# Prologue filler matmuls split into eight tiles of 64 rows by 32 columns, in a fused attention and MLP block

## The chip, the cores and the metric

The kernel runs on one core of one Trainium2 chip. The metric is the device time of one execution in microseconds, the median of three runs. A core has five engines that run their own instruction lists side by side and meet through semaphores: TensorE (PE in the profile; its weight loads are listed as PEld), VectorE (DVE), ScalarE (ACT), GpSimd (POOL) and SyncE (SP), which issues most DMAs. PE writes its results to PSUM, which has eight banks of 512 fp32 columns on 128 partitions; DVE and ACT read them from there. A matmul on PE is a pair of instructions: a weight load (LDWEIGHTS, the stationary operand) and the matmul itself, which streams the other operand through the array column by column.

## The reference

One layer norm feeds an attention with 32 query heads on one shared key and value head, and an MLP; both are added to the input.

```python
xn = _layernorm(x)                              # (1, 2048, 512), bf16
q = (xn @ wq).reshape(B, S, 32, 16)             # 32 heads of 16
k, v = xn @ wk, xn @ wv                         # one head of 16
p = softmax(q @ k.T * 16 ** -0.5)
a = (p @ v).reshape(B, S, 512) @ wo
h = gelu(xn @ w1 + b1)                          # 512 -> 1792
return x + a + h @ w2 + b2
```

## The kernel before

The kernel is straight-line code. Its functions do not issue instructions; they record operations with the tiles they read and write, a rough length and a due time (`Prog.add`). `Prog.schedule` then runs a planner: it simulates the engines, picks for each one the operation to put next, and so fixes the order of every engine's list; `Prog.emit` works out the semaphore waits and writes the lists. On the chip each engine works through its list in that order.

There are two parts in time.

The prologue (some 24 us) loads x in eight DMAs on SP's queue (line 770, two row tiles of 128 each), and behind them the weights wq, w1, w2. DVE and ACT take the statistics of the 16 row tiles (lines 851 to 877), DVE, ACT and POOL normalise them into `xn` (lines 887 and 891), PE transposes them (line 910, four transposes of 128x128 a tile), and ACT and DVE move the transposes from PSUM banks 0 to 2 to `xnT` (lines 915 and 917). From `xnT` PE projects K (line 741, 128x512, into bank 4), V and K in rows (line 741, 128x32, the kind "v") and the first query group (into bank 7). DVE's statistics are in a fixed list; a tile waits there for the DMA that brings it.

The body (all the rest) works through units of three score tiles: PE makes scores (line 1080, three row tiles of 32 rows), ACT takes their exponential (line 1104) or DVE makes an integer approximation of it (line 1135), and PE multiplies with V (line 1148, column tiles of 128 rows by 32 columns). The MLP and the projections are put into PE's gaps.

The fillers. While not all "v" matmuls of the prologue are placed, the planner puts a filler on PE where it has nothing else to place, from planner time 2.0 us on (`PRO_FROM`), as long as its count of PE activity in the last 3.413 us (`WIN`) is below 0.8 of that (`FILL_U`). It counts a filler as 0.107 us of activity, and as long as 0.107 us, or twice that while its model has PE slow. A filler multiplies a tile of zeros with itself and writes to PSUM bank 3, which nothing reads before line 1003. It waits for the zeros and for nothing else. The planner places 29 of them, in rows of 16, 9, 1, 1 and 2. In a later place of the body there are other fillers (line 1515 before), which the change does not touch.

Which instructions stand between the rows of fillers on PE: 4 transposes after the row of 16, 4 after the row of 9, 8 after the next one, 8 "v" matmuls after the next one, and after the last two the rest of the prologue, beginning with 8 transposes whose first waits for POOL.

Of the kernel before, what the change touches and what calls it, by code (L numbers as in the profile page):

```python
# [612 lines left out]
def bass_parallel_sum__grouped_kv_mqa__dense_activation_gelu__prompt_kernel(  # L613
# [33 lines left out]
    with ExitStack() as es:  # L647
        def sb(shape, dtype, name):
            return es.enter_context(nc.sbuf_tensor(name, shape, dtype))
# [20 lines left out]
        zeros = sb([P, P], bf, "zeros")  # L670
# [45 lines left out]
        def bank(b, n=1):  # L716
            return pAll[:, b * 512:(b + n) * 512]

        pO, pM = bank(6), bank(7)
        pr = Prog(nc)  # L720
# [53 lines left out]
        for i in range(8):  # L774
            e = X_Q[i]
# [734 lines left out]
        pr.in_chain = False  # L1510
        if PRO_FROM:
            zr = bass.AP(zeros[:].tensor, zeros[:].offset, [list(zeros[:].ap[0]), [0, 2], [1, P]])
            pr.pro_filler = lambda e: e.matmul(bank(3)[:, 0:256], zeros[:], zr, start=True, stop=True, skip_group_check=True)
        if FILL_GAP:
            pr.filler = lambda e, j, o: e.matmul((pO if o else pM)[32 * j:32 * j + 32, :], zeros[:, 0:32], xnT[:, 0, 0:TBW],
                                                 start=not o, stop=not o, skip_group_check=True,
                                                 tile_position=(0, 32 * j))
# [37 lines left out]
```

## Time and profile before

| | us |
|---|---|
| median of 3 runs | 730.26 (730.18 to 730.27) |
| the profiled execution | 730.02 |
| its span, first to last instruction | 728.2 |
| PE matmuls busy | 713.9 (98%) |
| PE weight loads busy | 223.5 (31%) |
| DVE busy | 691.4 (95%) |
| ACT busy | 712.8 (98%) |
| POOL busy | 418.2 (57%) |
| mean granted clock of PE | 0.997 |

A matmul's time in the profile runs from its start until its result is through, and matmuls overlap in the array, so a PE that is 98% busy is not full; start-to-start distances tell more. In the chain of waits each line is a start, a length and the work that the end of the kernel stood on at that time. In a timeline the bracket at a line's end is the idle time of that engine before it and what ended it. "PEclk", or the column before the DMA share in the table of windows, is the clock that PE was granted as a share of full speed. DMA queue q1 carries the transfers of SP, q8 and q14 instructions.

### The profile page before, as it was taken

To read this page: it belongs to the slowest core of one execution; us is meant where nothing else is said; L and a number is where in the kernel's file an instruction comes from. 1 tells how busy PE (TensorE), PEld (TensorE's weight loads), DVE (VectorE), ACT (ScalarE), POOL (GpSimd) and SP (SyncE) were. 2 spreads that over 40 slices of the span, in tenths; PEclk is the share of its full clock that TensorE was granted. 3 is DMA by queue.
4 is the path that set the end of the run, shared out by engine and by line. 5 is a ranking of instruction groups with operands and counts; after the bars stand their busy time and mean duration, and the time that the engine had idled before them with its cause. 6 is when DMAs were issued, how large, how long until landed. Compare 5 with 4: busy or idle time off the path is not lost.

```text
span 728.2 us, 22534 instructions
## 1 busy us (share of the span) xinstructions
PE 713.9 (98%) x9301; PEld 223.5 (31%) x9301; DVE 691.4 (95%) x1243; ACT 712.8 (98%) x757; POOL 418.2 (57%) x669
## 2 busy tenths in 40 slices
PE   7999999999999999999999999999999999999998
PEld 5333332232242323222222233222333222232332
DVE  8799999999999889999999999999999999999685
ACT  7899999999999999999999999999999999999997
POOL 8445567667665243667777754445663767755131
PEclk9999999999999999999999999999999999999999
DMA  9200101001010110110101021100101101011111
GB/s 312 72 13 18 29 9 25 17 13 29 9 40 9 28 44 18 23 34 10 30 14 32 14 48 30 28 20 9 29 7 25 27 22 25 16 40 32 26 29 39
DMA packets 36253, 23.59 MB, mean 32 GB/s; under 512 B 17768, under 2 KB 32568, under 8 KB 36152
## 3 DMA queue, kind: packets, MB, share of 16 engines
q1 hardware_dynamic: 35096, 22.12, 11.6%
q8 instruction: 74, 1.21, 0.7%
q14 instruction: 27, 0.22, 0.1%
q10 hardware_dynamic: 1056, 0.03, 0.1%
HBM read 13.28 MB, written 2.35 MB: 21 GB/s over the span
## 4 chain that ended last, share of the span: by engine, by line
ACT 55%; PE 37%; DVE 7%; DMA 1%; issue 0%; POOL 0%; SPq 0%
ACT E L1104 55%; PE pAll L1148 18%; PE pAll L1080 11%; PE pAll L765 4%; DVE Dt L1135 3%; PE pAll L747 2%; DVE Dt L1188 2%; PE pAll L741 1%; DVE stats L854 1%; DMA x_sb<-in_A_x_dram 1%; PE pAll L910 0%; PE pAll L761 0%; DVE x_sb L1314 0%; DVE qp L1280 0%; DVE Dt L1156 0%
## 5 line engine op out<-in xcount | busy, mean ns | idle before, releaser
L1104 ACT ACTIVATE E<-pAll 128x1024 bf16<-128x1024 f32 (+2 forms) x675 | 662.4, 1154 | 2.1 <-PE pAll L1080 0.6
L1155 POOL INT64_ADD Dt<-Dt x603 | 396.2, 666 | 289.9 <-DVE Dt L1135 116.2
L1135 DVE TENSOR_SCALAR Dt<-pAll 128x512 int16<-128x512 f32 (+2 forms) x570 | 394.1, 711 | 21.5 <-PE pAll L761 16.1
L1148 PE MATMUL pAll<-Dt,V 128*32 128x512 bf16 x3010 | 413.2, 383 | 0.7 <-DVE Dt L1188 0.2
L1148 PE MATMUL pAll<-E,V 128*32 128x512 bf16 x1446 | 280.1, 385 | 0.0
L1080 PE MATMUL pAll<-QT,KT 32*128 32x512 bf16 x2048 | 267.0, 384 | 5.3 <-ACT E L1104 3.6
L1188 DVE TENSOR_SCALAR Dt<-Dt 128x1024 int16<-128x1024 int16 (+4 forms) x302 | 202.4, 680 | 1.4 <-PE pAll L1148 0.7
L1080 PEld LDWEIGHTS pAll<-QT,KT 32*128 32x128 bf16 x2048 | 66.6, 90 | 273.9 <-ACT E L1104 246.7
L1148 PEld LDWEIGHTS pAll<-Dt,V 128*32 128x32 bf16 x3010 | 106.0, 94 | 114.0 <-issue 77.3
L1148 PEld LDWEIGHTS pAll<-E,V 128*32 128x32 bf16 x1446 | 65.5, 94 | 51.4 <-issue 39.7
L765 PE MATMUL pAll<-xnT,w_sb 128*32 128x512 bf16 x520 | 80.7, 383 | 0.3 <-DVE ub L1314 0.3
L1156 DVE TENSOR_SCALAR Dt<-Dt 128x1024 int16<-128x1024 int16 (+1 forms) x147 | 46.9, 341 | 0.1
L765 PE MATMUL pAll<-w_sb,x_sb 128*32 128x512 bf16 x304 | 46.5, 382 | 0.0
L765 PE MATMUL pAll<-w_sb,ub 128*32 128x512 bf16 x352 | 45.4, 382 | 0.0
L761 PE MATMUL pAll<-w_sb,ub 32*128 32x512 bf16 x96 | 36.9, 385 | 0.0
L765 PE MATMUL pAll<-wop,oTp 128*32 128x512 bf16 x192 | 34.9, 383 | 0.0
L761 PE MATMUL pAll<-w_sb,x_sb 32*128 32x512 bf16 x88 | 33.8, 384 | 0.1
L761 PE MATMUL pAll<-xnT,w_sb 32*128 32x512 bf16 x88 | 33.8, 384 | 0.1
L765 PEld LDWEIGHTS pAll<-xnT,w_sb 128*32 128x32 bf16 x520 | 20.3, 94 | 10.6 <-issue 6.8
L761 PE MATMUL pAll<-xnT,wq_sb 32*128 32x512 bf16 x60 | 23.1, 384 | 0.0
L1314 DVE TENSOR_SCALAR ub<-pAll,b1T 128x512 bf16<-128x512 f32 x28 | 20.6, 737 | 0.0
L747 PE MATMUL pAll<-xnT,w_sb 128*32 128x512 bf16 x288 | 20.3, 379 | 0.0
(135 smaller groups left out, 381.6 us busy)
## 6 DMA issues: line engine op xcount, KB each, us to landing
w_sb<-in_B_w_dram SPq DMA_DIRECT2D x2, 1792.0 KB, 13.3
OfP<-Of SPq DMA_DIRECT2D x96, 32.0 KB, 2.0
rbP<-rden_rows SPq DMA_DIRECT2D x96, 32.0 KB, 1.8
x_sb<-in_A_x_dram SPq DMA_DIRECT2D x8, 256.0 KB, 4.5
x_sb<-in_A_x_dram SPq DMA_DIRECT2D x16, 128.0 KB, 2.1
QT<-qp SPq DMA_DIRECT2D x124, 16.0 KB, 1.8
out_dram<-x_sb SPq DMA_DIRECT2D x15, 128.0 KB, 1.9
OfP<-Of SPq DMA_DIRECT2D x56, 16.0 KB, 1.8
```

What stands on the lines that cost most here:

```text
L741: return add("pe", lambda e: e.matmul(o, l, rh, start=start, stop=stop, **kw), r, w, occ=occ, lat=dlat[1], allow=allow, **ak)
L747: add("pe", lambda e, c=c, j=j: e.matmul(o[c, :], l[:, c], rh, start=start, stop=stop, tile_position=(0, 32 * j)), r, [(k, j) for k in w] ...
L761: add("pe", lambda e, b, c=c, j=j: e.matmul(pM, l[c, :], rh[c, :], start=False, stop=b, skip_group_check=True, tile_position=(32 * j, 0)), ...
L765: add("pe", lambda e, b, c=c, j=j: e.matmul(pM[c, :], l[:, c], rh, start=n == 0, stop=b, skip_group_check=True, tile_position=(0, 32 * j)) ...
L1080: ins = e.matmul(o, l, rh, start=True, stop=True, tile_position=(q0, 0))
L1104: o = act(lambda e: e.activation(E[:, s0:s0 + na, :], bank(b0, na).rearrange("p (a n) -> p a n", a=na), ACT.Exp, scale=LN2 / 128.0), w=[B( ...
L1135: op = dve(lambda e: e.tensor_scalar(Dt[:, s:s + n, :], bank(bk, n).rearrange("p (a n) -> p a n", a=n), float(127 * 128) + SPL_D, SPL_MIN, ...
L1148: add("pe", lambda e, a, b: e.matmul(pO[32 * j:32 * j + 32, :], V1[:, v, kt, :], rhs, start=a, stop=b, tile_position=(0, 32 * j)), r=r + [ ...
L1155: return e.int64_add(d.bitcast(dt.uint64), x.bitcast(dt.uint64), k * 0x0001000100010001 % 2 ** 64)
L1156: return e.tensor_scalar(d, x, float(k), None, ALU.add)
L1188: dve(lambda e, d=view(o, nb), q=view(i, nb), k=k: e.tensor_scalar(d, q, float(k), None, ALU.add), r=keys(i), w=keys(o), n=nb * n * TBW, m ...
L1314: dve(lambda e: e.tensor_scalar(ubs[tb % 2][:, ft, :], pM, b1T[:, ft:ft + 1], None, ALU.add), r=["b1T"], w=M4 + [ukey(tb, ft)], n=TBW + 57 ...
```

## The change

```diff
         if PRO_FROM:
             zr = bass.AP(zeros[:].tensor, zeros[:].offset, [list(zeros[:].ap[0]), [0, 2], [1, P]])
-            pr.pro_filler = lambda e: e.matmul(bank(3)[:, 0:256], zeros[:], zr, start=True, stop=True, skip_group_check=True)
+
+            def pro_filler(e):
+                for r0 in (0, 64):
+                    for c0 in (0, 32, 64, 96):
+                        ins = e.matmul((pM if r0 else bank(3))[c0:c0 + 32, 0:256], zeros[r0:r0 + 64, c0:c0 + 32], zr[r0:r0 + 64], start=True, stop=True,
+                                       skip_group_check=True, tile_position=(r0, c0))
+                return ins
+
+            pr.pro_filler = pro_filler
```

Each filler becomes eight matmuls, each on a tile of 64 rows by 32 columns of the array. The four tiles of the upper 64 rows write to the four groups of 32 partitions of bank 3, the four of the lower rows to those of bank 7 (`pM`). `zr` is the moving operand: the 128 columns of zeros, read twice, so 256 columns. The planner is not changed and still places 29 fillers in the same five rows; PE's list gets 232 matmuls in place of 29 and is the same in all else, and so are the lists of the other engines. Bank 7 is next written by the first query group, behind the last filler in PE's own order. Lines behind the change move by eight (1515 becomes 1523).

## The prediction

> **What bounds the kernel now.** I read the chain of waits for the whole span, then the same chain cut to the prologue, then PE's timeline, the windows with the granted clock, and last the DMA queues.
>
> ```profile
> span 728.2 us, 22534 instructions
> ...
> PE 713.9 (98%) x9301; PEld 223.5 (31%) x9301; DVE 691.4 (95%) x1243; ACT 712.8 (98%) x757; POOL 418.2 (57%) x669
> ...
> L1104 ACT ACTIVATE E<-pAll 128x1024 bf16<-128x1024 f32 (+2 forms) x675 | 662.4, 1154 | 2.1 <-PE pAll L1080 0.6
> ```
>
> From about 24 us on, the exponentials (ACT, line 1104) run with 2.1 us of waiting in all. The body is a full pipeline, so a prologue that ends later by some amount ends the kernel later by the same amount, and nothing behind 24 us can pay it back. The change touches only matmuls ahead of that. The prologue's chain, in order of time (start, length, what):
>
> ```profile
> 1.32 3.78 DMA x_sb<-in_A_x_dram
> ...
> 5.12 1.29 DVE stats L854 x2
> ...
> 11.36 0.76 POOL ub L891
> ...
> 12.17 0.62 PE pAll L910 x8
> ...
> 12.83 1.04 PE pAll L741 x4
> ...
> 24.11 0.92 ACT E L1104
> ```
>
> Up to 12.17 us the start is set by the loads of x, the statistics on DVE, and one normalisation on POOL. PE stands on it only from the transposes at 12.17. The fillers lie ahead of that:
>
> ```profile
> 1.05 3.39 PE L1513 MATMUL pAll<-zeros 128*128 128x256 bf16 x16 [1.05 <-POOL epsc L790]
> 7.50 0.61 PE L910 MATMUL pAll<-ident,ub 128*128 128x128 bf16 x4 [3.05 <-POOL ub L891]
> 7.90 2.13 PE L1513 MATMUL pAll<-zeros 128*128 128x256 bf16 x9
> 10.08 0.61 PE L910 MATMUL pAll<-ident,ub 128*128 128x128 bf16 x4
> 10.48 0.42 PE L1513 MATMUL pAll<-zeros 128*128 128x256 bf16 x1
> 10.91 0.62 PE L910 MATMUL pAll<-ident,ub 128*128 128x128 bf16 x8
> 11.37 0.27 PE L1513 MATMUL pAll<-zeros 128*128 128x256 bf16 x1
> 11.48 0.36 PE L741 MATMUL pAll<-wvk,xnT 128*128 128x32 bf16 x8
> 11.69 0.38 PE L1513 MATMUL pAll<-zeros 128*128 128x256 bf16 x2
> ```
>
> 29 fillers in five places. One takes (2.13-0.42)/8 = 0.21 us from start to start in the row of nine, and 0.38-0.27 = 0.11 us in the last row: half the clock, then the full one. What they buy is the clock (columns: window, length, busy time and count of PE, PEld, DVE, ACT, POOL, granted clock, DMA share, GB/s):
>
> ```profile
> 0.69:4.10 3.41, 3.05 (x15) 2.18 (x16) 1.68 (x4) 1.30 (x2) 2.58 (x17) 1.00 0.66 160
> 4.10:7.51 3.42, 0.36 (x4) 0.08 (x3) 3.26 (x8) 2.33 (x9) 3.20 (x8) 1.00 1.08 335
> 7.51:10.93 3.42, 3.35 (x19) 2.06 (x20) 3.42 (x12) 3.34 (x18) 3.42 (x12) 0.50 1.10 360
> 10.93:14.34 3.41, 3.27 (x44) 2.28 (x44) 3.41 (x9) 3.36 (x6) 3.01 (x13) 1.00 1.02 406
> ...
> 28.00:31.40 3.40, 3.03 (x34) 0.86 (x34) 2.76 (x6) 3.40 (x4) 0.00 (x0) 1.00 0.02 5
> ```
>
> A stretch of some 3.4 us in which PE idles (4.10 to 7.51) is followed by one at 0.50, and a busy stretch by one at 1.00. The full clock from 10.93 on is earned by the ten fillers and eight transposes of the stretch before.
>
> **The change part by part.** It removes 29 weight loads and 29 matmuls of 128 rows by 128 columns and adds 8 x 29 = 232 of each, of 64 rows by 32 columns, still with 256 columns streamed. The order of all else on PE is the same, with the same waits, and no other engine's list changes; the planner still thinks a filler is one full matmul.
>
> *Array time.* No 64x32 tile is in this trace. Its nearest rows are the column tiles and the row tiles of the body:
>
> ```profile
> 25.40 0.83 PE L765 MATMUL pAll<-xnT,wq_sb 128*32 128x512 bf16 x12
> ...
> 26.16 0.39 PE L1080 MATMUL pAll<-QT,KT 32*128 32x512 bf16 x3
> 26.17 0.38 PE L761 MATMUL pAll<-xnT,wq_sb 32*128 32x512 bf16 x1
> ...
> 26.49 0.39 PE L1148 MATMUL pAll<-E,V 128*32 128x512 bf16 x2
> ```
>
> Twelve column tiles of 0.38 to 0.39 us each end after 0.83 us, so four run as one, every (0.83-0.39)/2 = 0.22 us; three row tiles and a fourth take 0.39 us together. I take the eight to run as one: 0.21 us at half clock, 0.11 at full, plus 0.03 us once a row of fillers for their staggered starts (four starts lie within 0.01 us in the rows at 26.49 and 26.16). The lower bound is 0; the upper, if eight pairs come at the spacing of the 8 matmuls at 11.48, (0.36-0.18)/7 = 26 ns, is 0.21 us a filler, so 0.10 us more for each of the three at full clock.
>
> *Change of tiling.* Between row tiles and column tiles PE pauses: the row tiles start at 26.16, stream 512 columns for 0.22, and the column tiles start at 26.49, not 26.38, so 0.1 us. Today fillers and their neighbours are all full size and pay nothing. After the change each place pays 0.1 us going in and 0.1 coming out. Places one to three have room (idle until 7.50; the nine end near 9.82 and the transposes wait for their input until 10.08; the one at 10.48 ends at 10.70 against 10.91). Places four and five do not: 11.37+0.1+0.14+0.1 puts the eight matmuls at 11.71 instead of 11.48, their end at 11.91, and 0.1+0.24+0.1 later the transposes can start, 12.36 instead of 12.17. That 0.2 us is covered:
>
> ```profile
> 12.83 0.11 PEld L741 LDWEIGHTS pAll<-xnT,oTp 128*128 128x128 bf16 x2 [0.21 <-ACT xnT L915]
> ```
>
> ```profile
> 11.77 1.00 ACT L915 ACTIVATE xnT<-pAll 128x1024 bf16<-128x1024 bf16 x1
> ...
> 13.38 1.01 ACT L915 ACTIVATE xnT<-pAll 128x1024 bf16<-128x1024 bf16 x1
> ```
>
> The projection at 12.83 has waited 0.21 us for the eviction that ends at 12.77, and the eviction of the transposes themselves starts only at 13.38. So I put 0.0 us, with 0.3 for the upper bound above and up to 0.4 if a change of tiling costs twice as much at half clock; without the cover it is 0.2.
>
> *Instruction fetch.* This is the part that I expect to cost.
>
> ```profile
> q8 instruction: 74, 1.21, 0.7%
> ```
>
> ```profile
> q8 instruction: 1, 0.02, 7.5%
> ```
>
> ```profile
> 0.80 4.04 SPq L770 DMA_DIRECT2D x_sb<-in_A_x_dram  x8
> ```
>
>
> The first row is the whole span's, the second that of 18 to 19 us, the third the issue of the x loads.
> 74 packets of 16 KB are about one for every 251 of PE's 18,602 loads and matmuls, so this queue feeds PE. Over the first 18 us the queues' view has no q8 at all; its first packet is the one at 18 to 19 us, so PE starts with what it holds. The first row of fillers alone now has 256 instructions instead of 32. The first packet then falls at some 4 to 6 us, in the middle of the x loads, where all DMA engines are busy (share 1.08 above). 335 GB/s over 16 engines are 21 GB/s each, so 16 KB hold one of them for 0.78 us, and a load of x lands when its slowest engine is through. DVE has some margin: the eight loads are issued 0.5 us apart and land between 4.1 and about 9.7 (the rows of x_sb give 3.3 to 5.3 us from issue to landing), 0.8 us apart, while DVE's list comes to the sixth at 8.45:
>
> ```profile
> DMA to landing us min/median/max: 3.3/4.5/5.3
> ```
>
> ```profile
> 8.45 1.25 DVE L854 BATCH_NORM_STATS2 stats<-x_sb 128x6 f32<-128x512 bf16 x2
> ```
>
> Evenly spaced, the sixth lands near 8.1, a margin of some 0.35 us. 0.78-0.35 = 0.4 us is what I take, since the packet and the loads meet in the same engines; the bounds are 0 (it falls behind the loads, or on an engine that is ahead) and 0.8 (no margin). As DVE's delay moves POOL's normalisation, the 0.2 us of the transposes hides behind it too.
>
> [...]
>
> *Sum.* The profiled execution took 730.02 us: 728.2 span and 1.8 around it; 728.2 + 0.4 + 1.8 = 730.4. The median of the runs is 730.26, so the forecast is 730.26 + 0.4 = **730.7 us**. Its own range is 730.1 to 731.6.
>
> **The rivals.** *PE is not supplied fast enough* (slower). 232 pairs of load and matmul in place of 29, through one in-order queue. The densest long stretch of the trace:
>
> ```profile
> 208.00:215.00 7.00, 7.00 (x124) 2.78 (x112) 7.00 (x9) 6.60 (x6) 4.84 (x7) 1.00 0.17 38
> 17.32:20.32 3.00, 2.94 (x62) 2.42 (x60) 2.26 (x6) 2.25 (x5) 2.10 (x3) 1.00 1.10 346
> ```
>
> That is 56 ns a pair over 7 us and 48 over 3 us. Eight such are 0.45 us a filler, four times the array time. Ahead of the transposes of 12.17 stand 232 + 24 = 256 pairs; 256 x 0.056 = 14.3 us from 1.05 is 15.4, 3.2 late, 3.0 after the cover: 733.3 (with 48 ns, 1.2 late, 731.3). It decides as soon as a pair costs over some 45 ns. Against it stand the bursts of 26 ns, though these may have been fetched ahead; nothing in the trace runs long at the rate that is now asked. 13%.
>
> [...]
>
> *The clock is not earned.* If small tiles count less as activity, 7.51 to 10.93 no longer earns the full clock, and one more stretch of 3.4 us runs at half, which costs at most 1.7 us: 730.7 + 1.7 = 732.4, 734 for two. Against it: the row 28.00:31.40 has only tiles and keeps 1.00. It keeps it, though; it doesn't regain it. 13%.
>
> *The halves run after each other* (the change doesn't do what it says). The four tiles of rows 0 to 63 and the four of rows 64 to 127 share column groups. A filler is then 0.43 us cold, 0.22 warm; the nine end near 11.4 instead of 9.82, and with the pauses the transposes of 12.17 start near 13.8: 1.5 late after the cover, 731.8. Three row tiles over the same columns at 26.16 speak against it. 8%; all eight in a row (over 10 us) 3%.
>
> *Faster.* Only if longer fillers keep the clock up through 4.10 to 7.51; the matmuls that gain from it, at 7.50 to 10.91, stand on no chain. 6%.
>
> **How the numbers follow.** Forecast 57%, the rest as above. A measurement of this kernel tells no change from about 0.2%, that is 1.5 us, so within 728.8 to 731.7 counts as the same: the forecast's 57%, less 3 for its tail, with 3 from the supply rival at 48 ns: 57%. Slower: 37%. Faster: 6%. The range must leave out the cases over 10 us and two cold stretches, and take in the supply rival: 729.9 to 733.5.
>
> **What would show it.** Right: 232 matmuls of 64 rows by 32 columns, each place as long as before within 0.1 us, the clock at 1.00 from the same stretch on, a packet on q8 before 7 us, a wait of DVE for x between 6 and 9 us, and the first exponential 0 to 0.8 us later. Wrong: transposes of 12.17 waiting for fillers (supply, or halves: the spacing of the small matmuls tells which), a clock of 0.50 after 10.93, or a shift behind 24 us that differs from that at the first exponential.

## The result, and the profile after

| | before | after |
|---|---|---|
| median of 5 runs, us | 730.19 (730.00 to 730.27) | 732.64 (732.42 to 733.59) |
| the profiled execution, us | 730.02 | 732.49 |
| its span, us | 728.2 | 730.7 |
| first exponential (line 1104), us from the span's start | 24.01 | 26.43 |

The changed kernel is slower: ratio 1.0036, 95% interval 1.0021 to 1.005, or 2.45 us between the medians. The shift is complete at the first exponential: 26.43 - 24.01 = 2.42 us there, 730.7 - 728.2 = 2.5 us at the end.

From the page of the changed kernel, the span, the exponentials and the instruction queue:

```profile
span 730.7 us, 22937 instructions
...
q8 instruction: 76, 1.25, 0.7%
...
L1104 ACT ACTIVATE E<-pAll 128x1024 bf16<-128x1024 f32 (+2 forms) x675 | 662.4, 1155 | 2.2 <-PE pAll L1080 0.6
```

The body is what it was: 662.4 us of exponentials with 2.2 us of waiting before them, against 662.4 and 2.1. Two more packets have come on q8. Where the first of them falls is in the view of the DMA queues, cut to 5 to 10 us:

```profile
q8 instruction: 1, 0.02, 1.5%
```

One packet, busy for 1.5% of 16 engines' 5 us, which is 1.2 us of one engine. DVE's timeline shows what lies beside it (start, length, what; in brackets the idle time before and what ended it):

```profile
7.01 0.66 DVE L854 BATCH_NORM_STATS2 stats<-x_sb 128x6 f32<-128x512 bf16 x1
9.31 0.69 DVE L854 BATCH_NORM_STATS2 stats<-x_sb 128x6 f32<-128x512 bf16 x1 [1.64 <-DMA x_sb<-in_A_x_dram]
```

DVE now stands 1.64 us for the fifth load of x, where before it went from tile to tile. The chain of waits, cut to the prologue, has that load as its longest piece:

```profile
2.83 6.45 DMA x_sb<-in_A_x_dram
...
9.31 0.69 DVE stats L854
...
11.76 0.61 PE pAll L910 x4
12.37 0.34 PE pAll L1517 x7
12.71 0.97 PE pAll L910 x8
13.68 0.34 PE pAll L1517 x6
14.03 0.33 PE pAll L741 x8
14.36 0.56 PE pAll L1517 x14
14.91 0.94 PE pAll L910 x8
15.88 1.02 ACT xnT L915
```

The second group of transposes starts at 11.76 instead of 10.08 (+1.68), the ones that were at 12.17 start near 14.85 (+2.68), the first exponential at 26.43 (+2.42). Between these two profiles there are two pieces: 1.68 us in front of the second transposes, and 2.42 - 1.68 = 0.74 us behind them. Fillers (line 1517) and their neighbours now stand on the chain. PE's timeline gives the spacing:

```profile
1.05 3.61 PE L1517 MATMUL pAll<-zeros 64*32 64x256 bf16 x128 [1.05 <-POOL epsc L790]
7.39 0.40 PE L910 MATMUL pAll<-ident,ub 128*128 128x128 bf16 x4 [2.73 <-POOL ub L891]
7.72 1.18 PE L1517 MATMUL pAll<-zeros 64*32 64x256 bf16 x72
11.76 0.61 PE L910 MATMUL pAll<-ident,ub 128*128 128x128 bf16 x4 [2.87 <-DVE ub L891]
12.30 0.41 PE L1517 MATMUL pAll<-zeros 64*32 64x256 bf16 x8
12.64 1.04 PE L910 MATMUL pAll<-ident,ub 128*128 128x128 bf16 x8
13.61 0.41 PE L1517 MATMUL pAll<-zeros 64*32 64x256 bf16 x8
13.96 0.40 PE L741 MATMUL pAll<-wvk,xnT 128*128 128x32 bf16 x8
14.29 0.63 PE L1517 MATMUL pAll<-zeros 64*32 64x256 bf16 x16
14.85 1.00 PE L910 MATMUL pAll<-ident,ub 128*128 128x128 bf16 x8
```

Nine fillers, 72 small matmuls, now end after 1.18 us at the full clock (2.13 us at half clock before). If the last one takes 0.27 us, as a filler at full clock did, a filler has (1.18 - 0.27)/8 = 0.114 us: the array time of the old one. The windows show the clock (window, length, busy time and count of PE, PEld, DVE, ACT, POOL, granted clock, DMA share, GB/s):

```profile
2.02:5.43 3.41, 2.65 (x104) 1.72 (x88) 2.03 (x4) 2.34 (x5) 3.01 (x15) 1.00 1.03 269
5.43:8.84 3.41, 1.45 (x76) 1.12 (x76) 2.24 (x6) 2.21 (x10) 3.41 (x13) 1.00 1.08 359
8.84:12.25 3.41, 0.54 (x12) 0.34 (x4) 2.94 (x10) 1.89 (x10) 2.43 (x7) 0.50 1.07 384
12.25:15.67 3.42, 3.42 (x58) 2.28 (x57) 3.42 (x10) 2.86 (x7) 2.54 (x10) 0.50 1.04 392
15.67:19.08 3.41, 3.31 (x46) 2.27 (x45) 3.17 (x8) 3.20 (x13) 1.65 (x4) 1.00 1.08 347
```

In the trace the clock's records begin at 5.43 here: 1.00 for 3.41 us, 0.50 for 6.83 us, then 1.00. In the profile of before they begin at 4.10: 1.00 for 3.41 us, 0.50 for 3.41 us, then 1.00. The limits at 2.02 and 12.25, where no record changes, are an estimate in steps of 3.41 us from these. Ahead of 5.43 the column's 1.00 is no reading: (3.61 - 0.42)/15 = 0.21 us a filler in the first row is the spacing at half clock. The stretch from 2.02 holds small fillers alone (2.65 us of work) and is followed by one at 1.00. From 8.84 to 12.25 PE has 0.54 us of work, since the late tile holds up the transposes; the clock is 0.50 there and in the stretch behind it, up to 15.67. In the profile of before, it was back at 10.93. The stretches of the two profiles lie differently (their limits are at 8.84 and 12.25 here, at 7.51 and 10.93 there), and what that alone is worth is taken up behind the data packets below.

### The profile page after: what moved, and what is told of

Read it like the earlier page. It is cut to its first block, busy times and chain, and to the rows that moved or that the text cites. A ratio compares the mean times of both kernels' runs of the same rounds, so it can differ in the third digit from the quotient of the medians.

```text
span 730.7 us, 22937 instructions
## 1 busy us (share of the span) xinstructions
PE 713.7 (98%) x9501; PEld 224.2 (31%) x9504; DVE 692.0 (95%) x1243; ACT 712.8 (98%) x757; POOL 417.5 (57%) x669
## 3 DMA queue, kind: packets, MB, share of 16 engines
q8 instruction: 76, 1.25, 0.7%
## 4 chain that ended last, share of the span: by engine, by line
ACT 55%; PE 37%; DVE 6%; DMA 1%; issue 0%; SPq 0%; POOL 0%
ACT E L1104 55%; PE pAll L1148 18%; PE pAll L1080 11%; PE pAll L765 4%; DVE Dt L1135 3%; PE pAll L747 2%; DVE Dt L1188 2%; DMA x_sb<-in_A_x_dram 1%; PE pAll L910 1%; PE pAll L741 0%; ACT xnT L915 0%; PE pAll L761 0%; DVE stats L854 0%; SPq L770 0%; DVE x_sb L1314 0%
## 5 line engine op out<-in xcount | busy, mean ns | idle before, releaser
L1104 ACT ACTIVATE E<-pAll 128x1024 bf16<-128x1024 f32 (+2 forms) x675 | 662.4, 1155 | 2.2 <-PE pAll L1080 0.6
```

What stands on the lines that cost most here:

```text
L1104: o = act(lambda e: e.activation(E[:, s0:s0 + na, :], bank(b0, na).rearrange("p (a n) -> p a n", a=na), ACT.Exp, scale=LN2 / 128.0), w=[B( ...
```

## The experiments

Two theories to start with. *Fetch*: more instructions on PE bring the first packet of q8 forward into the loads of x, one engine's share of a load comes late, and DVE waits; the shape of the fillers does not matter. *Tiling*: changing between full and small tiles, the spacing of the small ones or a clock they do not earn costs the time; their number does not matter. Unless noted, an experiment was run ten times ("first row, again" nine) beside 19 to 25 runs of the kernel before, whose medians were 730.16 to 730.23.

Two tables stand ahead, both read from the traces in the same way for all kernels. Each load of x lands in sixteen shares. The first table takes the records of the DMA transfers: when the first packet of 16 KB left and how long it took, the first load of x of which one share came late (landing of the last share but one, and of the last), and DVE's wait for that load. In the kernel before, the last share lands 0.1 us behind the one before it, in each of the eight loads. The records do not name the DMA engine, so that the late share is that of the packet's engine is inferred from the times.

| kernel | packet leaves | takes | load | last share but one, last | DVE waits |
|---|---|---|---|---|---|
| after | 6.22 | 1.23 | fifth | 7.28, 9.29 | 1.64 |
| after, once more | 6.30 | 0.88 | fifth | 7.51, 8.99 | 1.18 |
| columns | 5.62 | 1.81 | fifth | 7.47, 9.24 | 1.47 |
| first row, once | 5.91 | 1.34 | fourth | 6.48, 7.69 | 0.55 |
| first row, again | 6.30 | 1.73 | fourth | 6.70, 9.12 | 1.99 |
| filled wait | 5.69 | 2.12 | fourth | 6.71, 9.27 | 2.11 |
| twelve | 7.47 | 1.11 | sixth | 8.06, 9.69 | 1.24 |
| late rows | 13.06 | 1.11 | none | 0.26 apart at most | 0 |
| four tiles | 11.99 | 1.09 | none | | 0 |
| data packet, early | 4.10 | 0.76 | none | 0.29 apart at most | 0 |
| data packet, later | 8.70 | 0.68 | none | | 0 |

The second gives the starts of the second transposes, of those that were at 12.17, and of the first exponential, and the shift of each from the kernel before (10.08, 12.17, 24.01).

| kernel | second transposes | later transposes | first exponential |
|---|---|---|---|
| after | 11.76 (+1.68) | 14.85 (+2.68) | 26.43 (+2.42) |
| after, once more | 11.47 (+1.39) | 14.55 (+2.38) | 25.98 (+1.97) |
| columns | 11.72 (+1.64) | 14.09 (+1.92) | 26.37 (+2.36) |
| late rows | 10.11 (+0.03) | 13.20 (+1.03) | 25.83 (+1.82) |
| four tiles | 10.05 (-0.03) | 13.10 (+0.93) | 24.43 (+0.42) |
| first row, once | 11.40 (+1.32) | 13.72 (+1.55) | 25.62 (+1.61) |
| first row, again | 12.19 (+2.11) | 14.51 (+2.34) | 26.86 (+2.85) |
| filled wait | 12.66 (+2.58) | 14.35 (+2.18) | 26.29 (+2.28) |
| twelve | 11.38 (+1.30) | 14.46 (+2.29) | 26.46 (+2.45) |
| data packet, early | 10.06 (-0.02) | 12.58 (+0.41) | 25.03 (+1.02) |
| data packet, later | 10.02 (-0.06) | 12.54 (+0.37) | 25.00 (+0.99) |

**Columns: the count without the tiles.** Each filler as eight matmuls on the full array, of 32 columns each.

```diff
-                for r0 in (0, 64):
-                    for c0 in (0, 32, 64, 96):
-                        ins = e.matmul((pM if r0 else bank(3))[c0:c0 + 32, 0:256], zeros[r0:r0 + 64, c0:c0 + 32], zr[r0:r0 + 64], start=True, stop=True,
-                                       skip_group_check=True, tile_position=(r0, c0))
+                for c0 in range(0, 256, 32):
+                    ins = e.matmul(bank(3)[:, c0:c0 + 32], zeros[:], zeros[:, 0:32], start=True, stop=True, skip_group_check=True)
```

> Fetch (232 pairs bring PE's first instruction packet into the x loads, one DMA engine falls 2 us behind, DVE waits): the same number of PE instructions as in the changed kernel and no tiles at all, so a packet on q8 near 6 us, a wait of DVE for x of 1.3 to 2.0 us, 732.0 to 732.8 us. Tiling (changes of tiling, or small tiles that are slow or earn no clock): nothing of it is left, 730.1 to 730.4 us.

732.55 us, ratio 1.0043 (1.0021 to 1.0065). DVE's timeline has the same wait at the same tile:

```profile
9.27 0.69 DVE L854 BATCH_NORM_STATS2 stats<-x_sb 128x6 f32<-128x512 bf16 x1 [1.47 <-DMA x_sb<-in_A_x_dram]
```

Without a single small tile the time is that of the changed kernel, 0.1 us apart. Tiling falls as the main cause. (The profiled execution of this run took 740.18 us, at a mean granted clock of 0.950 that begins at 16 us. DVE's wait and the transposes lie before that; the first exponential in the table, 26.37, lies behind it and is therefore no typical one. The median is hardly touched by one execution of ten.)

**Late rows: the tiles without the early count.** The first 16 fillers stay full, the other 13 are split.

```diff
+            placed = [0]
+
             def pro_filler(e):
+                placed[0] += 1
+                if placed[0] <= 16:
+                    return e.matmul(bank(3)[:, 0:256], zeros[:], zr, start=True, stop=True, skip_group_check=True)
                 for r0 in (0, 64):
```

> Only the last 13 fillers are tiled, the first row of 16 is as before. Fetch: PE's 256th instruction comes at about 11.5 us and the packet at about 13 us, behind the x loads; no wait of DVE for x behind the first load, 730.2 to 730.8 us. Tiling: all places that cost something (rows two to five) are still tiled, 731.0 to 732.6 us. If small tiles earn no clock, the clock stays at half through 11 us whatever the phase.

730.4 us, ratio 1.0008 (0.9998 to 1.0017): no difference that this measurement can tell. The packet leaves at 13.06, behind the loads of x, and DVE does not wait. All the changes of tiling on the chain are in this kernel, so they are not what costs 2.45 us. Its profiled execution, at 733.18 us, is the slowest of the ten. Its matmuls run at half clock up to some 16.6 us and once more at 26.9 to 30.3 us; its 25.83 for the first exponential is therefore no typical one.

**First row: the early count without the later tiles.** The reverse of it, run twice.

```diff
+                placed[0] += 1
+                if placed[0] > 16:
+                    return e.matmul(bank(3)[:, 0:256], zeros[:], zr, start=True, stop=True, skip_group_check=True)
                 for r0 in (0, 64):
```

> Only the first row of 16 is tiled, the last 13 are full matmuls as before. Fetch: packet near 6 us, DVE's wait for x 1.3 to 2.0 us, 731.6 to 732.6 us. Tiling: the first row has 2.7 us of idle time behind it, so nothing, 730.1 to 730.5 us.

733.61 us from four runs (731.57 to 733.88), ratio 1.0048 (1.0032 to 1.0065). DVE's wait is there, in two pieces of 0.55 and 0.54 us. The spread of 2.3 us over four runs was too wide to price anything, so it was run again, in one set with "filled wait" below.

> The kernel with only the first row tiled, once more, as the one to set the next beside: 731.6 to 733.9 us, packet near 6 us, DVE waiting for x 1 to 2 us.

732.18 us (731.27 to 733.02), ratio 1.0026 (1.0016 to 1.0036), with a wait of 1.99 us:

```profile
9.14 1.29 DVE L854 BATCH_NORM_STATS2 stats<-x_sb 128x6 f32<-128x512 bf16 x2 [1.99 <-DMA x_sb<-in_A_x_dram]
```

The first row alone makes most of the loss or all of it, while the other 13 fillers alone make none that shows. The wait varies from run to run with the load that is hit.

**Four tiles: half the count.** Each filler as four column tiles of 128 rows by 32 columns, so 128 instructions in the first row.

```diff
-                for r0 in (0, 64):
-                    for c0 in (0, 32, 64, 96):
-                        ins = e.matmul((pM if r0 else bank(3))[c0:c0 + 32, 0:256], zeros[r0:r0 + 64, c0:c0 + 32], zr[r0:r0 + 64], start=True, stop=True,
-                                       skip_group_check=True, tile_position=(r0, c0))
+                for c0 in (0, 32, 64, 96):
+                    ins = e.matmul(bank(3)[c0:c0 + 32, 0:256], zeros[:, c0:c0 + 32], zr, start=True, stop=True,
+                                   skip_group_check=True, tile_position=(0, c0))
```

> Every filler as four column tiles of 128 rows by 32 columns: tiled in all five places, half the instructions. Fetch: the 256th instruction of PE at about 11.5 us, packet near 13 us, 730.2 to 730.8 us. Tiling: the same ten changes of tiling as in the changed kernel, 731.5 to 732.7 us.

730.35 us, ratio 1.0004 (0.9995 to 1.0013). The packet leaves at 11.99 and DVE does not wait. PE's timeline shows what the changes of tiling cost without the collision:

```profile
10.05 0.61 PE L910 MATMUL pAll<-ident,ub 128*128 128x128 bf16 x4
10.59 0.40 PE L1516 MATMUL pAll<-zeros 128*32 128x256 bf16 x4
10.93 1.03 PE L910 MATMUL pAll<-ident,ub 128*128 128x128 bf16 x8
11.89 0.40 PE L1516 MATMUL pAll<-zeros 128*32 128x256 bf16 x4
12.23 0.39 PE L741 MATMUL pAll<-wvk,xnT 128*128 128x32 bf16 x8
12.55 0.62 PE L1516 MATMUL pAll<-zeros 128*32 128x256 bf16 x8
13.10 0.69 PE L910 MATMUL pAll<-ident,ub 128*128 128x128 bf16 x8
```

From 10.05 to 13.10 are 3.05 us, as long as in the changed kernel (14.85 - 11.76 = 3.09), against 2.32 in "first row, again", where the same transposes stand between full fillers, also at half clock. Six changes of tiling (in and out of three rows) thus cost 3.05 - 2.32 = 0.7 us at this place, 0.12 each. Of this, at most 0.42 us arrives at the first exponential, and in the median 0.2 us, which the interval does not tell from nothing.

**Filled wait: the clock alone.** As "first row", but 14 more full fillers in the second row, so that PE is busy while DVE waits.

```diff
                 if placed[0] > 16:
-                    return e.matmul(bank(3)[:, 0:256], zeros[:], zr, start=True, stop=True, skip_group_check=True)
+                    for _ in range(15 if placed[0] == 25 else 1):
+                        ins = e.matmul(bank(3)[:, 0:256], zeros[:], zr, start=True, stop=True, skip_group_check=True)
+                    return ins
```

> As before with only the first row tiled, but the second row has 23 full fillers in place of 9, so that PE stays busy while x is late. If part of the loss is a clock that falls while PE waits for the late x: the same packet and the same wait of DVE, but the transposes of 12.17 come at full clock, and the time is 0.5 to 2 us below the run beside it, 731.0 to 732.0 us. If all of the loss is the late x: as the run beside it within 0.3 us.

731.76 us (731.05 to 732.23), ratio 1.0018 (1.0009 to 1.0028), against 732.18 of "first row, again" in the same set. PE's timelines, this kernel first and "first row, again" second:

```profile
7.91 4.92 PE L1520 MATMUL pAll<-zeros 128*128 128x256 bf16 x23
12.66 0.39 PE L910 MATMUL pAll<-ident,ub 128*128 128x128 bf16 x4
...
14.35 0.62 PE L910 MATMUL pAll<-ident,ub 128*128 128x128 bf16 x8
```

```profile
7.87 2.13 PE L1519 MATMUL pAll<-zeros 128*128 128x256 bf16 x9
12.19 0.61 PE L910 MATMUL pAll<-ident,ub 128*128 128x128 bf16 x4 [2.19 <-DVE ub L891]
...
14.51 1.06 PE L910 MATMUL pAll<-ident,ub 128*128 128x128 bf16 x8
```

With PE kept busy the four transposes take 0.39 us instead of 0.61 and the eight 0.62 instead of 1.06: the full clock is back when they start. (The clock column says 1.00 throughout for both kernels; its records begin late or are missing there, so the clock is read from these lengths.) Behind the second transposes this kernel makes up 2.58 - 2.28 = 0.30 us, where "first row, again" loses 2.85 - 2.11 = 0.74. Some of this is its own doing: DVE has the input of the second transposes ready at 12.44 here and at 12.13 there, and the added fillers let them start 0.22 us behind it instead of 0.06. From that input to the first exponential it is 13.85 us here and 14.73 there, 0.88 us apart. The medians differ by 0.42 us only and the two intervals overlap, so the price of the clock stays between about 0.4 and 0.9 us by this pair.

**Data packet, early and later: the cause without the instructions.** The kernel before, with one copy of 16 KB in a single piece, from the weights to a tile that nothing uses yet, issued by ACT: first at its start, then behind its first statistic. Early:

```diff
+        add("act", lambda e: e.dma_start(E[0:1, 0:16, :].rearrange("p a n -> p (a n)"), B_w2.rearrange("f d -> (f d)")[0:8192].rearrange("(o n) -> o n", o=1)),
+            w=[("E", i) for i in range(16)], dma="d_pad", occ=0.0, lat=2.2, due=0.02, after=[tload])
```

> The kernel before with its 29 full fillers, and one more transfer of 16 KB in one piece, from w2 to a buffer that is not yet in use, issued by ACT at about 3.2 us. If one 16 KB packet on one DMA engine is what makes x late: that engine's share of the x loads lands 0.8 to 2 us behind the other fifteen, DVE waits 0.4 to 1.7 us, 730.6 to 732.5 us. If it is something else about instruction fetch (a transfer of data gives way, or is spread over the engines): no wait, 730.1 to 730.4 us.

730.42 us, ratio 1.0001 (0.9992 to 1.0011). It left at 4.10, ahead of most loads. From the third load on, one share is 0.28 us behind the others; DVE did not wait. Whether the packet does even that is not shown, since "late rows" has such a share too (0.26 us), with no packet so early. It left earlier than meant, hence the later one.

```diff
-                    act(lambda e, ti=ti, c=c: e.activation(scr, x_sb[:, ti, :], ACT.Identity, accum_out=sm[:, c:c + 1]),
+                    o = act(lambda e, ti=ti, c=c: e.activation(scr, x_sb[:, ti, :], ACT.Identity, accum_out=sm[:, c:c + 1]),
...
+                    if ti == 1:
+                        add("act", lambda e: e.dma_start(E[0:1, 0:16, :].rearrange("p a n -> p (a n)"), B_w2.rearrange("f d -> (f d)")[0:8192].rearrange("(o n) -> o n", o=1)),
+                            w=[("E", i) for i in range(16)], dma="d_pad", occ=0.0, lat=2.2, due=-1.0, after=[o])
```

> The kernel before with its full fillers and one more transfer of 16 KB in one piece, as in the run with the early packet (which left at 4.10 us, ahead of the full load on the DMA engines, and held its engine back by only 0.3 us), now issued by ACT at about 5 us, so that it leaves at about 7 us. If a 16 KB packet on a fully loaded DMA engine is what makes x late: one share of the x loads lands 0.8 to 2 us behind the others, DVE waits 0.3 to 1.7 us for it, 730.6 to 732.3 us. If only instruction packets do that: no wait, 730.1 to 730.5 us.

730.2 us, ratio 0.9999 (0.999 to 1.0009). ACT's timeline has the issue:

```profile
4.97 0.49 ACTq L854 DMA_DIRECT2D E<-in_B_w_dram  x1
```

It left at 8.70 instead of the 7 us that were meant, took 0.68 us among the last loads, and no share came late. So DVE waited for neither data packet, while q8's packets, where they fell among the loads, took 0.9 to 2.1 us and put one share 1.2 to 2.6 us back. But neither data packet left between 5.6 and 7.5 us, as the harmful ones of q8 did, and the later one met only the last two loads. That a data packet would be harmless there is not shown, nor why those of q8 weigh more. These two kernels show something else, though. Nothing of the change is in them, but their profiled executions (730.98 and 731.03 us) reach the first exponential 1.0 us late. The windows of the earlier one:

```profile
5.40:8.83 3.43, 1.38 (x13) 1.02 (x13) 3.38 (x11) 2.51 (x11) 3.43 (x13) 0.98 1.09 353
8.83:15.65 6.82, 5.57 (x42) 3.89 (x43) 6.66 (x18) 5.78 (x16) 5.79 (x19) 0.51 1.05 387
15.65:19.00 3.35, 3.35 (x56) 2.69 (x54) 2.99 (x7) 3.00 (x16) 1.78 (x3) 1.00 1.10 348
```

The half clock lasts 6.8 us, one stretch longer than in the profile of before, and ends at 15.53. The kernel before does the same in some executions: in one set of 24, all seven with a mean clock of 0.995 took 730.57 to 731.08 us, and all 17 with 0.997 or more 729.83 to 730.42. (Two stretches of 3.41 us at half clock make 0.995 over the whole span, one makes 0.998.) One more stretch at half clock is worth some 0.8 us here.

This bears on the 0.74 us of the changed kernel. The stretches of the earlier one of these kernels fall within 0.15 us of those of the changed kernel, no load is late in it, and its half clock lasts as long: from 8.83 to 12.24 PE has 2.16 us of work, and the stretch behind that is at half as well. Beside it the changed kernel's first exponential comes 26.43 - 25.03 = 1.40 us later, less than DVE's wait of 1.64. In the same way, the executions of the changed kernel with a mean clock of 0.995 took 732.01 to 732.49 us, 1.0 to 1.5 us more than the seven above, whose median is 730.97. So where the stretches fall like this, the late load alone makes the loss, and the 0.74 us are the difference of two placements. With another placement it does cost a stretch. PE's work in "first row, again", and in "four tiles", where nothing is late (the clock column is not to be used here, as the records of both begin later; the limits are an estimate, counted back in steps of 3.41 us from where the matmuls' lengths change, near 17.0 and 13.3):

```profile
10.12:13.54 3.42, 1.35 (x12) 1.29 (x13) 3.42 (x13) 2.75 (x13) 1.85 (x6) 1.00 1.04 399
```

```profile
9.89:13.30 3.41, 3.41 (x43) 1.97 (x40) 3.41 (x9) 3.08 (x10) 3.41 (x11) 1.00 1.05 395
```

Behind the first, eight transposes still take 1.06 us and four projections 1.81; behind the second, four projections take 1.03, the length at full clock.

**After, once more.** The changed kernel unaltered, to see how far its profile repeats.

> The changed kernel once more, for where the clock's stretches fall: packet near 6 us and DVE's wait of 1.3 to 2 us again, as nothing in them depends on the clock; the clock's full stretch may begin anywhere from 10 to 17 us, and the first exponential between 25.5 and 27 us with it.

732.01 us in its one execution: the packet at 6.30, the fifth load late, the half clock up to 15.0, the first exponential at 25.98.

**Twelve: the packet moved.** The first four fillers full, the other 25 split, so 200 instructions in the first row instead of 256.

```diff
+                placed[0] += 1
+                if placed[0] <= 4:
+                    return e.matmul(bank(3)[:, 0:256], zeros[:], zr, start=True, stop=True, skip_group_check=True)
                 for r0 in (0, 64):
```

> The changed kernel with the first 4 of its 29 fillers as full matmuls, the other 25 as eight tiles: 200 small matmuls in place of 232, all five places still tiled. Fetch: PE's first row and the four transposes behind it now end at 208 instructions, short of the point at which the first packet is asked for, and PE waits there until 7.4 us; so the packet leaves behind 8.5 us, when all but the last two x loads are through, DVE waits not at all or under 0.5 us, 730.2 to 730.9 us. If the number of small matmuls, their tiling or their supply is what costs: 25/29 of the changed kernel's loss is left, 732.1 us or more.

732.24 us (731.18 to 732.79), ratio 1.0022 (1.0013 to 1.0032). By its time alone this is the branch of the other theory (732.1 or more); against that stand "late rows" and "four tiles", which keep the later rows tiled and lose nothing that shows. The packet left at 7.47, sooner than expected, when PE had started some 205 instructions. But it moved, by 1.25 us, and the late load with it, from the fifth to the sixth:

```profile
7.01 1.25 DVE L854 BATCH_NORM_STATS2 stats<-x_sb 128x6 f32<-128x512 bf16 x2
...
9.72 1.29 DVE L854 BATCH_NORM_STATS2 stats<-x_sb 128x6 f32<-128x512 bf16 x2 [1.24 <-DMA x_sb<-in_A_x_dram]
```

The tile that waited 1.64 us in the changed kernel is taken without a wait here, and the next one waits 1.24. Packet and late share go together.

No kernel here beat the one before; "late rows", "four tiles" and the two with a data packet equal it.

## Why the prediction was right in kind, and too small

The forecast was 730.7 us and the median 732.64: a loss of 2.45 us where 0.4 was forecast. The mechanism that made the forecast is the one at work; its size was wrong. The forecast's own range, 730.1 to 731.6, ends 1.0 us short of the result. The wide range of 729.9 to 733.5 holds it only because it was widened for the rival of PE's supply (733.3), which fell; that it holds is luck. The result lies on the slower side, which got 37% and not 57%.

- **Instruction fetch, forecast +0.4 us, measured +1.68 at the second transposes.** Two of the signs named for it came: a packet on q8 before 7 us (6.22), and DVE waiting for x, from 7.67 to 9.31. The third, a first exponential at most 0.8 us later, did not (2.42). The step that failed is "16 KB hold one of them for 0.78 us". That was worked out from the mean rate of 21 GB/s, while the row quoted beside it, 7.5% of 16 engines over 1 us, says 1.2 us for such a packet; with it the sum would have been 1.2 - 0.35 = 0.85 us. Even that is short: the share came 9.29 - 7.28 = 2.0 us late. The margin was right: 7.67 - 7.28 = 0.39 us for the fifth load, and 2.0 - 0.39 = 1.62 is the wait of 1.64 us. The upper bound of 0.8 us fell with the same step. The prediction had a price for the packet's length alone, and none for how late the share comes.
- **Fetch, the engine and the loads beside it.** For the engine that fetches, the trace shows no loss, as far as it goes: the packet is under way from 6.22 to 7.45 us, and the transposes behind the 256th instruction start at 7.39, where before they started at 7.50, and wait for POOL both times. For the loads beside it, the runs show one: "columns" and "first row" lose 1.95 to 3.45 us with DVE waiting for a load of which a share comes late.
- **Clock, forecast no change, measured from nothing to one stretch at half clock (some 0.8 us), by execution.** The sign that was named, 0.50 after 10.93, came. The rival that it belonged to (small tiles count less as activity) has little for it: small tiles alone, 2.65 us of work in 3.41, were followed by 1.00 at 5.43. One stretch stays unexplained: in "late rows" PE is busy for 3.38 of 3.42 us from 9.81 to 13.23 (limits estimated, counted back in steps of 3.41 us from 16.6), in part with small tiles, and runs at half clock behind it (eight transposes take 1.04 us, four projections 1.91). What the prediction left out is that the late load idles PE (0.54 us of work in a stretch of 3.4). Whether that costs a stretch depends on where the stretches fall: in "first row, again" it did, in the profile of the changed kernel the same stretch is at half clock without a late load too ("data packet, early"). So 1.68 + 0.74 = 2.42 us describes two profiles and is no sum of two effects. Of the 2.45 us of the medians, 1.0 to 1.5 are left where the clock is the same. The rest fits one stretch that the kernel before pays in seven executions of 24 only; this split is worked out from a few executions, not shown by an experiment of its own.
- **Change of tiling, forecast 0.1 us a change and 0.0 in the sum.** The price is right: 0.12. The six changes behind the second transposes make the later transposes 0.7 us later, twice the bound of 0.3 to 0.4, since the row between the second and third transposes, which had slack in the old schedule, is on the chain when the tile is late or the clock is half. But 0.0 in the sum agrees with the medians: "columns", with none of these changes, has 732.55 us, the changed kernel 732.64, and "four tiles", with all of them, loses 0.2 us that can't be told from nothing.
- **Array time, forecast 0.** Right: 0.114 us a filler at full clock.
- **Rivals that fell.** PE's supply: 72 pairs of load and matmul at full clock in 0.114/8 = 14 ns each, not 48 to 56. Halves one after the other: a filler would take 0.22 us at full clock, it takes 0.114, half of that.
- **The body pays nothing back.** Right: 2.42 us at the first exponential, 2.5 at the end.

What stays open is why an instruction packet delays a share by more than its own length in five of seven traces, when the data packets of the same size on ACT's queue delayed no load that DVE waited for. A data packet between 5.6 and 7.5 us, or on the loads' own queue, was not tried.

## What to carry to other kernels

Count instructions, not only busy time, when a change multiplies them: work that costs no engine anything can still move an instruction packet into a burst of loads (from 18.42 to 6.22 us here), and the load that is on the critical path pays (1.64 us of waiting). Price such a packet from its own row in the trace, not from the mean bandwidth, and leave room above it: 1.2 us of packet put a share 2.0 us back here. Follow the wait that it makes to the end, since a PE that idles can lose its clock too (1.35 us of work in 3.42 in "first row, again", and eight transposes took 1.06 us behind it, not 0.62), and compare profiles only where the half-clock stretches lie alike. If many small instructions are wanted ahead of critical loads, keep the count low enough that the next packet falls behind the loads; with 128 in the first row (packet at 11.99 us, 730.35 us), or with the first row left whole (13.06 us, 730.4 us), no loss against 730.16 us showed.

## What the runs showed of the hardware

- Where packets of 16 KB on q8 left between 5.6 and 7.5 us, beside the loads of x, they took 0.9 to 2.1 us, and one share of sixteen came 1.2 to 2.6 us late; it stayed back in all the loads behind it (in the changed kernel the fifth to the eighth). Data packets of 16 KB on ACT's queue, at 4.10 and 8.70 us, took 0.76 and 0.68 us, and no share was more than 0.29 us behind (0.26 in "late rows", with no packet so early).
- The first packet left when PE had started some 205 instructions ("twelve", 7.47 us), 251 ("four tiles", 11.99), 258 (the changed kernel, 6.22) and 291 ("late rows", 13.06).
- Eight tiles of 64 by 32 took as long as one full matmul (0.114 us a filler at full clock, 0.11 before), and a stretch that held them alone, 2.65 us in 3.41, was followed by one at 1.00.
- One stretch more at half clock costs this kernel some 0.8 us, and the same kernel has it in some executions and not in others (seven of 24).
- One execution of "columns" had a granted clock of 0.950 instead of 0.99 or more from 16 us to its end, and took 740.18 us instead of some 732.5.
